# Attention and two dense blocks on one core: scores as three products of rounded parts from the eighth job on

## The chip, the cores and the metric

One core of a Trainium2 chip runs the whole kernel. The metric is the device time of one execution in microseconds (us). The engines are named as the profile names them: PE (TensorE, with its weight loads as PEld), DVE (VectorE), ACT (ScalarE), POOL (GpSimd) and SP (SyncE, which issues most of the transfers). Each engine works through its own instructions in the order in which the program holds them.

## The reference

```python
scores = scale * np.matmul(q, k.transpose(0, 1, 3, 2))        # 4 batches, 8 heads, 576 x 64
thresh = np.max(scores, axis=-1, keepdims=True) - tau
scores = np.where(scores >= thresh, scores, -1000000000.0)
scores = scores - np.max(scores, axis=-1, keepdims=True)
attn = np.exp(scores)
attn = attn / (np.sum(attn, axis=-1, keepdims=True) + 1e-09)
x = np.matmul(attn, v)                                         # then 2304 tokens x 512
h = x @ w_in                                                   # 512 x 2048
g = np.where(h >= 1, h, np.where(h <= -1, 0.0, (h + 1) ** 2 / 4.0))
x = g @ w_out                                                  # 2048 x 512
h = x @ w_in2
out = (h * np.clip(h + 3.0, 0.0, 6.0) / 6.0) @ w_out2
```

All inputs are float32. Which scores pass the threshold depends on small differences between them, so they are computed to nearly full float32 accuracy.

## The kernel before

**Attention.** There are 16 jobs, one for each batch and pair of heads. A job has five blocks of query rows: four of 128 rows, and a last one that holds the 64 remaining rows of both heads. `em_scores` computes a block: for each head and each half of the 576 keys one matmul, whose contraction is the 64 rows of a head, so head 0 uses rows 0 to 63 of the PE array and head 1 rows 64 to 127. These four matmuls (line 328) are plain float32, and the trace records each as two MATMULs. DVE evicts the scores negated, with their maximum (line 341), ACT takes the exponential (line 353), DVE masks and sums (line 362), PE turns the block over by multiplying with the identity (line 277), ACT copies that back (line 390), and PE multiplies with v (line 426).

**q and k.** A matmul wants the 64 head dimensions on the partitions. For the first four jobs (`j < JT`, `JT = 4`) PE turns q and k over, and ACT copies them out of PSUM with the scale (lines 294, 309). From the fifth job on the transfers write strips of 32 elements, so that one DVE transpose of 32 x 32 squares finishes the work (lines 286, 302), and POOL multiplies q by the scale (line 288). `qt` and `kt` have two buffers each, and the scheduler that orders the program places their making a job ahead.

**Dense work.** Matmuls of the dense blocks are three products of rounded parts: an operand is split into `hi` (rounded to the type float32r) and `lo` (the rest, also float32r), and hi·hi, hi·lo and lo·hi are added up in PSUM. Each product is one MATMUL. Weights are loaded as 512 KB tiles (`w_raw`, line 96 and 99) and rounded and split by ACT, DVE and POOL (`split_a`, `split_b`, lines 118 to 141).

**Beside attention.** As soon as the first batch is done, a generator (`part1`) feeds pieces of the first dense block between the pieces of attention: 256 tokens at a time, for the first `NF1 = 10` of 16 inner blocks (lines 666 and 728). Each piece of attention earns `share = 0.57` of credit and a third of a step costs 0.33. The rest of the first block and the whole second block follow after attention, mostly 512 tokens at a time (lines 666 and 708). In attention there are `RAW + MORE = 5` buffers for raw weights.

Of the kernel before, what the change touches and what calls it, by code (L numbers as in the profile page):

```python
# [8 lines left out]
F32 = mybir.dt.float32  # L9
F32R = mybir.dt.float32r  # L10
ACTF = mybir.ActivationFunctionType
ALU = mybir.AluOpType
# [6 lines left out]
def kernel(  # L19
# [13 lines left out]
    V, S, G, T = nc.vector, nc.scalar, nc.gpsimd, nc.tensor  # L33
    NB, NH, SEQ, D = q.shape
# [4 lines left out]
    MAIN = 512  # L39
    TAIL = SEQ - MAIN  # L40
    HS = SEQ // 2
# [3 lines left out]

    WIDE = [MAIN] * NB + [NB * TAIL]
    NW = len(WIDE)
    NF1 = 10
    NAT = 1
    JT = 4  # L50
    MLAG = 2
    RAW = 3
    MORE = 2

    const = ctx.enter_context(tc.tile_pool(name="const", bufs=1))
    wbase = ctx.enter_context(tc.tile_pool(name="wbase", bufs=1))
# [7 lines left out]
    taus = const.tile([128, 4], F32, name="taus")  # L64
# [9 lines left out]
    def f32(ap):  # L74
        return ap.bitcast(F32)
# [26 lines left out]
    def after(ins, prev, sync=False):  # L102
        if prev is not None:
            kind = mybir.DependencyClass.Sync if sync else mybir.DependencyClass.NoSync
            why = mybir.DependencyReason.ANTI if sync else mybir.DependencyReason.DATA
            tc.add_manual_dep(ins.ins, prev.ins.name, mybir.DependencyInfo(kind, why), reason="pace")

    pe_pins = []
    pins = {"S": None, "V": None, "G": None}

    def split_a(kind, m, f):
        t = wraw.pop((kind, m, f))
        pool = wbase if f < NF1 else wpool[f]
        hi = pool.tile([128, 512], F32R, tag=f"w{kind}h{f}", name=f"w{kind}h{f}")
# [91 lines left out]
    ap = att_es.enter_context(tc.tile_pool(name="att", bufs=1))  # L206
    mode = {"mlp": False, "att": True, "step": False, "t": 0, "s": 0, "n": 0}

    qn = ap.tile([128, 5, 128], F32, name="qn")
    kn = ap.tile([128, 5, 128], F32, name="kn")  # L210
    vn = [ap.tile([128, 5, 2, D], F32, name=f"vn{i}") for i in range(2)]
    qt, kt = {}, {}
    rp = ap.tile([128, 32], F32, name="rp")
    rq = ap.tile([128, 32], F32, name="rq")
    G.memset(rp, 0.0)
# [13 lines left out]

    def load_q(j):  # L230
        if j >= NJ:
            return
        E = nc.sync if j else nc.scalar
        b, hp = jobs[j]
        for h in HEADS:
            src = q[b, 2 * hp + h]
            if j >= JT:
                strips(qn, 0, src, h)
                continue
            E.dma_start(out=qn[:, 0:4, h * D:(h + 1) * D], in_=rows(src, b))  # L240
            E.dma_start(out=qn[0:TAIL, 4, h * D:(h + 1) * D], in_=src[MAIN:SEQ, :])

    def load_k(j):
# [23 lines left out]
    readers = {}  # L267
# [5 lines left out]
    def reads(x, ago=0):  # L273
        readers[(mode["s"] - ago) % 2] = x

    def turn(out, in_, pin):
        x = T.transpose(out, in_, ident)  # L277
        if pin:
            pe_pins.append(x)

    def unit_q(j):
        if j >= NJ or j in qt:
            return
        qt[j] = ap.tile([128, SEQ], F32, tag="qt", name="qt", bufs=2)
        if j >= JT:
            V.transpose(out=qt[j], in_=qn.rearrange("p c n -> p (c n)")[:, 0:SEQ])
            load_q(j + 1)
            G.tensor_scalar(out=qt[j], in0=qt[j], scalar1=taus[:, 1:2], scalar2=None, op0=ALU.mult)
            return
        tm = unit_bank().rearrange("p e n -> p (e n)")  # L290
        for c in range(5):
            turn(tm[:, c * 128:(c + 1) * 128], qn[:, c, :], c == 0)
        load_q(j + 1)
        reads(S.activation(out=qt[j], in_=tm[:, 0:SEQ], func=ACTF.Copy, scale=taus[:, 1:2]))

    def unit_k(j):

        if j >= NJ or j in kt:
            return
        kt[j] = ap.tile([128, SEQ + TAIL], F32, tag="kt", name="kt", bufs=2)  # L300
        if j >= JT:
            V.transpose(out=kt[j], in_=kn.rearrange("p c n -> p (c n)"))
            load_k(j + 1)
            return
        tm = unit_bank().rearrange("p e n -> p (e n)")
        for i, c in enumerate((4, 0, 1, 2, 3, 4)):
            turn(tm[:, i * 128:(i + 1) * 128], kn[:, c, :], i == 0)
        load_k(j + 1)
        reads(S.activation(out=kt[j], in_=tm[:, 128 - TAIL:128 + MAIN + TAIL], func=ACTF.Copy))
# [4 lines left out]
    def em_scores(j, i):  # L314

        last = i == NBLK - 1

        if not last:
            mode["s"] += 1
        ss = [unit_bank() for _ in range(1 if last else 2)]  # L320
        prev = None
        c = slice(i * 128, i * 128 + (TAIL if last else 128))
        for x, (h, e) in enumerate(((0, 0), (1, 1), (0, 1), (1, 0)) if last else ((0, 0), (1, 0), (0, 1), (1, 1))):
            r = slice(h * D, (h + 1) * D)
            k0 = e * HS + (TAIL if last or h == 0 else 0)
            o = ss[0][h * TAIL:(h + 1) * TAIL, e, 0:HS] if last else ss[h][:, e, 0:HS]
            with tc.high_priority(offset=900 if x else 0):
                mm = T.matmul(o, qt[j][r, c], kt[j][r, k0:k0 + HS], start=True, stop=True, skip_group_check=True)  # L328
            after(mm, prev)
            prev = mm  # L330
            if x == 0:
                pe_pins.append(mm)
                for y in range(1 if last else 2):
                    after(mm, readers.get((mode["s"] - y) % 2), True)
        nm = ap.tile([128, 2], F32, tag="nm", name="nm", bufs=3)
        th = ap.tile([128, 2], F32, tag="th", name="th", bufs=3)
        p = ap.tile([128, 2, 2, HS], F32, tag="p", name="p", bufs=3)
        if i == 0:
            zt[j] = ap.tile([128, 9], F32, tag="z", name="z", bufs=2)
        for x, s in enumerate(ss):  # L340
            reads(V.tensor_scalar(out=p[:, x], in0=s[:, :, 0:HS], scalar1=-1.0, scalar2=3e38,  # L341
                                           op0=ALU.mult, op1=ALU.min, accum_out=nm[:, x:x + 1]), len(ss) - 1 - x)
        blk[j, i] = (p, nm, th, [])

# [416 lines left out]
    def fin_out(g, a, i):  # L761
# [7 lines left out]
        if c < nmain:  # L769
            b, r = divmod(c, MAIN // 128)  # L770
            if b >= NAT or JT < HP:
                dst = out[b * SEQ + r * 128:b * SEQ + r * 128 + 128, :]
# [5 lines left out]
                b = (c - nmain) * 2 + e  # L778
                nc.sync.dma_start(out=out[b * SEQ + MAIN:(b + 1) * SEQ, :], in_=ob[64 * e:64 * e + 64, :])

    HALF = NF1 // 2
    ROUNDS = [(g, list(range(f, f + HALF))) for f in (0, HALF) for g in range(2)]
    ROUNDS += [(g, list(range(NF1))) for g in range(2, NG)]
    before = {}
    hs = [(r, f) for r, (g, fs) in enumerate(ROUNDS) for f in fs]
    n_h = len(hs)
    outs = [(r, half, f) for r, (g, fs) in enumerate(ROUNDS) for half in range(2) for f in fs]
    OFF = NF1 + 2 * MLAG - 3
    steps, o = [], 0
    while o < len(outs):  # L790
        n = len(steps)
# [94 lines left out]
    V.tensor_scalar(out=taus[:, 3:4], in0=taus[:, 2:3], scalar1=0.0, scalar2=3e38, op0=ALU.is_lt, op1=ALU.mult)  # L886
    V.tensor_scalar(out=taus[:, 1:2], in0=taus[:, 2:3], scalar1=0.0, scalar2=0.125, op0=ALU.is_ge, op1=ALU.mult)
    V.tensor_tensor(out=taus[:, 0:1], in0=taus[:, 2:3], in1=taus[:, 3:4], op=ALU.max)
    warm = [None]

    def warm_up(n):
# [13 lines left out]

    fs1 = list(range(NF1))
    fs2 = list(range(NF1, KF))
    first_use = {("i", f): f for f in fs1}
# [15 lines left out]
            weights.half()  # L924

    part1 = dense1(ready, ahead1)
    share = 0.57
    FIRST, RATE = 5, 0.85
    credit = 0.0
    for _ in attention():  # L930
        if not mode["mlp"]:
            if mode["t"] == 3:
                weights.prefetch()
            if mode["t"] >= 5 and mode["step"]:
                mode["step"] = False
                if weights.done < FIRST and mode["t"] % 5 in (0, 4):
                    weights.half()
            if not ready(0):
                continue
            mode["mlp"] = True  # L940
        credit = min(credit + share, 3.0)
        while credit > 0:
            c = next(part1)
            if c is None:
                break
            credit -= c
# [95 lines left out]
```

## Time and profile before

| | |
|---|---|
| median of 3 runs | 1124.33 us (1123.8 to 1125.87) |
| profiled execution | 1126.53 us, of which the span from the first to the last instruction is 1124.7 us |
| granted TensorE clock, mean | 0.994 of full speed |
| first scores of job 6, 7 and 8 (counted from 0) | about 138, 180 and 218 us |
| first dense matmul beside attention | about 112 us |
| last score matmul, last work of attention | about 457 us, about 477 us |

The span has four parts: attention alone (to 110 us), attention with dense work beside it (to 477 us), the rest of the first dense block (to about 800 us) and the second one. A busy time is the union of an engine's instructions. MATMULs overlap each other, so the time that one takes from the stream is the distance from its start to the next start, and not its own length.

### The profile page before, as it was taken

To read this page: it belongs to the slowest core of one execution; us is meant where nothing else is said; L and a number is where in the kernel's file an instruction comes from. 1 tells how busy PE (TensorE), PEld (TensorE's weight loads), DVE (VectorE), ACT (ScalarE), POOL (GpSimd) and SP (SyncE) were. 2 spreads that over 40 slices of the span, in tenths; PEclk is the share of its full clock that TensorE was granted. 3 is DMA by queue.
4 is the path that set the end of the run, shared out by engine and by line. 5 is a ranking of instruction groups with operands and counts; after the bars stand their busy time and mean duration, and the time that the engine had idled before them with its cause. 6 is when DMAs were issued, how large, how long until landed. Compare 5 with 4: busy or idle time off the path is not lost.

```text
span 1124.7 us, 17618 instructions
## 1 busy us (share of the span) xinstructions
PE 1086.1 (97%) x6478; PEld 881.8 (78%) x6478; DVE 586.9 (52%) x1204; ACT 614.3 (55%) x1215; POOL 435.5 (39%) x382
## 2 busy tenths in 40 slices
PE   7988779999999999999999999999999999999998
PEld 5555557778887778888889888888888888898886
DVE  5788979876666666256535855657410211211111
ACT  5677777776666666565657766645422322333222
POOL 1133667632212221246636666568622222222221
PEclk9999999999999999999999999999999999999999
DMA  6353535433222210015322444543110110010001
GB/s 166 95 117 79 135 102 157 121 73 87 63 59 64 55 39 24 12 49 169 94 85 85 132 147 153 153 128 102 35 38 1 34 38 1 10 38 6 14 1 38
DMA packets 140422, 84.26 MB, mean 75 GB/s; under 512 B 99632, under 2 KB 123440, under 8 KB 140336
## 3 DMA queue, kind: packets, MB, share of 16 engines
q1 hardware_dynamic: 138976, 82.84, 26.8%
q8 instruction: 51, 0.84, 0.3%
q10 hardware_dynamic: 1360, 0.30, 0.1%
q14 instruction: 35, 0.29, 0.1%
HBM read 65.73 MB, written 17.37 MB: 74 GB/s over the span
## 4 chain that ended last, share of the span: by engine, by line
PE 86%; DVE 6%; ACT 3%; DMA 2%; issue 1%; POOL 1%; SPq 1%; ACTq 0%; DVEq 0%; POOLq 0%
PE Q L666 35%; PE P L708 28%; PE Q L728 7%; PE P L328 6%; PE Q L426 5%; PE Q L277 5%; DVE p L341 2%; DVE p L362 2%; ACT e L353 1%; DMA qn<-in_q_dram 1%; DMA w_raw<-in_moe_w_in_dram 0%; DMA rb<-rd 0%; DVE w_c L135 0%; ACT Gf L390 0%; SPq L227 0%
## 5 line engine op out<-in xcount | busy, mean ns | idle before, releaser
L684 POOL TENSOR_TENSOR gl<-r,gh 128x512 fp32r<-128x512 f32 (+1 forms) x190 | 202.4, 1065 | 508.3 <-ACT gh L683 506.4
L666 PE MATMUL Q<-xh,wih 128*128 128x512 f32 (+1 forms) x760 | 262.7, 346 | 6.9 <-DVE r L677 6.0
L666 PE MATMUL Q<-xh,wil 128*128 128x512 f32 (+1 forms) x760 | 257.6, 339 | 0.0
L666 PE MATMUL Q<-xl,wih 128*128 128x512 f32 (+1 forms) x760 | 257.5, 339 | 0.0
L680 DVE SCALAR_TENSOR_TENSOR r<-r,Q 128x512 f32<-128x512 f32 (+1 forms) x80 | 50.7, 634 | 249.3 <-ACT r L679 249.2
L683 ACT ACTIVATE gh<-r 128x512 fp32r<-128x512 f32 (+1 forms) x190 | 99.9, 526 | 128.5 <-PE P L708 52.3
L666 PEld LDWEIGHTS Q<-xh,wih 128*128 128x128 f32 x760 | 144.6, 190 | 31.4 <-DVE r L677 8.2
L666 PEld LDWEIGHTS Q<-xl,wih 128*128 128x128 f32 x760 | 144.6, 190 | 15.8
L666 PEld LDWEIGHTS Q<-xh,wil 128*128 128x128 f32 x760 | 144.5, 190 | 15.3
L341 DVE TENSOR_SCALAR_CACHE_REDUCE p<-P 128x576 f32<-128x576 f32 x144 | 103.9, 751 | 54.4 <-PE Q L277 39.1
L362 DVE SCALAR_TENSOR_TENSOR p<-p,th,e 128x576 f32<-128x576 f32 x144 | 123.6, 879 | 15.4 <-ACT e L353 9.6
L679 ACT ACTIVATE r<-Q,three 128x512 f32<-128x512 f32 (+1 forms) x80 | 51.5, 643 | 143.7 <-PE Q L666 140.5
L353 ACT ACTIVATE e<-p,nm 128x576 f32<-128x576 f32 x144 | 108.5, 774 | 29.2 <-DVE p L341 28.3
L677 DVE SCALAR_TENSOR_TENSOR r<-r,Q 128x256 f32<-128x256 f32 (+1 forms) x110 | 54.9, 499 | 120.2 <-ACT r L676 117.0
L277 PE MATMUL Q<-ident,p 128*128 128x128 f32 x656 | 108.5, 284 | 7.8 <-ACT Gf L390 4.3
L328 PE MATMUL P<-kt,qt 64*128 64x288 f32 (+1 forms) x640 | 99.4, 429 | 14.7 <-DVE p L341 13.8
L708 PE MATMUL P<-woh,gh 128*128 128x512 f32 x288 | 111.9, 390 | 0.6 <-DVE ob L766 0.6
L708 PE MATMUL P<-wol,gh 128*128 128x512 f32 x288 | 112.2, 390 | 0.0
L708 PE MATMUL P<-woh,gl 128*128 128x512 f32 x288 | 111.0, 390 | 0.0
L277 PEld LDWEIGHTS Q<-ident,p 128*128 128x128 f32 x656 | 74.5, 142 | 44.2 <-issue 11.8
L137 POOL TENSOR_TENSOR w_c<-w_c,w_raw 128x512 int32<-128x512 int32 x64 | 88.7, 1387 | 41.7 <-DVE w_c L135 21.8
L390 ACT ACTIVATE Gf<-Q 128x512 f32<-128x512 f32 x128 | 74.2, 595 | 34.4 <-PE Q L277 33.6
(91 smaller groups left out, 1834.3 us busy)
## 6 DMA issues: line engine op xcount, KB each, us to landing
w_raw<-in_moe_w_in_dram SPq DMA_DIRECT2D x32, 512.0 KB
w_raw<-in_moe_w_out_dram SPq DMA_DIRECT2D x32, 512.0 KB
vn<-in_v_dram SPq DMA_DIRECT2D x32, 128.0 KB
x2p<-ob SPq DMA_DIRECT2D x16, 256.0 KB
x2d<-ob SPq DMA_DIRECT2D x16, 256.0 KB
xst<-x2d SPq DMA_DIRECT2D x16, 256.0 KB
out_dram<-ob SPq DMA_DIRECT2D x16, 256.0 KB
xst<-xd SPq DMA_DIRECT2D x15, 256.0 KB
```

The lines of the kernel that those rows point to most:

```text
L137: x = G.tensor_tensor(out=c.bitcast(I32), in0=c.bitcast(I32), in1=r, op=ALU.add)
L277: x = T.transpose(out, in_, ident)
L328: mm = T.matmul(o, qt[j][r, c], kt[j][r, k0:k0 + HS], start=True, stop=True, skip_group_check=True)
L341: reads(V.tensor_scalar(out=p[:, x], in0=s[:, :, 0:HS], scalar1=-1.0, scalar2=3e38, op0=ALU.mult, op1=ALU.min, accum_out=nm[:, x:x + 1]), ...
L353: pins["S"] = S.activation(out=e, in_=p[:, x], func=ACTF.Exp, bias=nm[:, x:x + 1], scale=-1.0)
L362: V.scalar_tensor_tensor(out=p[:, x], in0=p[:, x], scalar=th[:, x:x + 1], in1=e, op0=ALU.is_le, op1=ALU.mult, accum_out=zt[j][:, z:z + 1])
L390: S.activation(out=f[:, h, :, d0:d0 + 128], in_=tm.rearrange("p (c n) -> p c n", c=4), func=ACTF.Copy)
L666: mm = T.matmul(h, l[:, kk * 128:(kk + 1) * 128], r, start=(x == 0), stop=(x == 3 * KD - 1))
L683: x = S.activation(out=gh, in_=r, func=ACTF.Copy)
L684: y = G.tensor_tensor(out=gl, in0=r, in1=f32(gh), op=ALU.subtract)
L708: T.matmul(a, l, r, start=(first and x == 0), stop=(last and x == 2))
L728: mm = T.matmul(o, l, r, start=(f == fs[0] and x == 0 and i == 0), stop=(f == fs[-1] and x == 2 and i == 1), skip_group_check=True)
```

## The change

From the eighth job on (`JT = 7`) the scores are three products too. `split_t` lets DVE transpose the strips into `raw` (one buffer), ACT copy that into the rounded part (`qt`, `kt`, now float32r), and POOL subtract to get `ql` and `kl`. A block then is 12 MATMULs instead of 4 float32 matmuls. The last block of such a job is done for both heads at once: the 64 rows of head 0 and of head 1 stand in q on the diagonal of a 128 x 128 square whose other half is zero, so six MATMULs with all 128 rows do it. The scale moves into the eviction (`scalar1 = taus[:, 3:4]`), and POOL's multiplication falls away. Jobs 4 to 6 (counted from 0) now take the way over PE that jobs 0 to 3 took. Nine inner blocks instead of ten run beside attention, in rounds of 4 and 5, with a share of 0.52, and there is one buffer less for raw weights.

```diff
-    NF1 = 10
+    NF1 = 9
-    JT = 4
+    JT = 7
-    MORE = 2
+    MORE = 1
...
             if j >= JT:
-                strips(qn, 0, src, h)
+                strips(qn, 0, src[0:MAIN, :], h)
+                strips(qn, 16 + 2 * h, src[MAIN:SEQ, :], h)
                 continue
...
+    def split_t(nat, hi, name):
+        raw = ap.tile([128, SEQ + TAIL], F32, tag="raw", name="raw")
+        lo = ap.tile([128, SEQ + TAIL], F32R, tag=name, name=name, bufs=2)
+        V.transpose(out=raw, in_=nat.rearrange("p c n -> p (c n)"))
+        S.activation(out=hi, in_=raw, func=ACTF.Copy)
+        G.tensor_tensor(out=lo, in0=raw, in1=f32(hi), op=ALU.subtract)
+        return lo
...
         if j >= JT:
-            V.transpose(out=qt[j], in_=qn.rearrange("p c n -> p (c n)")[:, 0:SEQ])
+            ql[j] = split_t(qn, qt[j], "ql")
             load_q(j + 1)
-            G.tensor_scalar(out=qt[j], in0=qt[j], scalar1=taus[:, 1:2], scalar2=None, op0=ALU.mult)
             return
...
         if j >= JT:
-            V.transpose(out=kt[j], in_=kn.rearrange("p c n -> p (c n)"))
+            kl[j] = split_t(kn, kt[j], "kl")
...
+        terms = ((qt, kt), (qt, kl), (ql, kt)) if thirds else ((qt, kt),)
+        for pair in (((0, 0),), ((0, 1),)) if whole else (es[0:2], es[2:4]):
+            for n, (a, w) in enumerate(terms):
+                for h, e in pair:
+                    r = slice(0, 128) if whole else slice(h * D, (h + 1) * D)
...
-            reads(V.tensor_scalar(out=p[:, x], in0=s[:, :, 0:HS], scalar1=-1.0, scalar2=3e38,
+            reads(V.tensor_scalar(out=p[:, x], in0=s[:, :, 0:HS],
+                                           scalar1=taus[:, 3:4] if j >= JT else -1.0, scalar2=3e38,
...
-    HALF = NF1 // 2
-    ROUNDS = [(g, list(range(f, f + HALF))) for f in (0, HALF) for g in range(2)]
+    HALF = 4
+    ROUNDS = [(g, list(range(a, z))) for a, z in ((0, HALF), (HALF, NF1)) for g in range(2)]
...
-    share = 0.57
+    share = 0.52
```

**Order on PE.** First block of the eighth job; P are the score banks of the two heads. Before:

```order
L328 MATMUL P_2359<-kt,qt 128x288
L328 MATMUL P_2360<-kt,qt 128x288
L328 MATMUL P_2359<-kt,qt 128x288
L328 MATMUL P_2360<-kt,qt 128x288
L666 MATMUL Q_2073<-xh,wih_1311 128x256
```

Now:

```order
L349 MATMUL P_2357<-kt,qt 128x288
L349 MATMUL P_2358<-kt,qt 128x288
L349 MATMUL P_2357<-kl,qt 128x288
L349 MATMUL P_2358<-kl,qt 128x288
L349 MATMUL P_2357<-kt,ql 128x288
L349 MATMUL P_2358<-kt,ql 128x288
L349 MATMUL P_2357<-kt,qt 128x288
L349 MATMUL P_2358<-kt,qt 128x288
L349 MATMUL P_2357<-kl,qt 128x288
L349 MATMUL P_2358<-kl,qt 128x288
L349 MATMUL P_2357<-kt,ql 128x288
L349 MATMUL P_2358<-kt,ql 128x288
```

The two heads still alternate, and a bank gets its three products one pair after the other.

**Order on DVE.** Around the last block of the eighth job, where q and k of a later job are made (L341 and L364 are evictions, L362 and L386 masks). Before:

```order
L677 SCALAR_TENSOR_TENSOR r<-r,Q_2424 128x256
L356 TENSOR_SCALAR th<-nm,taus 128x2
L362 SCALAR_TENSOR_TENSOR p,z<-p,th,e 128x576 x2
L286 STREAM_TRANSPOSE qt<-qn 128x576
L302 STREAM_TRANSPOSE kt<-kn 128x640
L341 TENSOR_SCALAR p,nm<-P_2709 128x576
```

Now:

```order
L364 TENSOR_SCALAR p,nm<-P_2749,taus 128x576
L701 SCALAR_TENSOR_TENSOR r<-r,Q_2333 128x256
L380 TENSOR_SCALAR th<-nm,taus 128x1
L285 STREAM_TRANSPOSE raw<-kn 128x640
L386 SCALAR_TENSOR_TENSOR p,z<-p,th,e 128x576
```

The transpose of k no longer follows that of q at once: the transpose of q stands before this piece, and the one of k behind the eviction, with the mask behind it.

**Order on POOL.** At that place, for q and k of the same job. Before:

```order
L141 TENSOR_TENSOR wol_2592<-w_c,woh_2591 128x512
L122 TENSOR_SCALAR w_c<-w_c 128x512
L288 TENSOR_SCALAR qt<-qt,taus 128x576
L684 TENSOR_TENSOR gl<-r,gh 128x256
L137 TENSOR_TENSOR w_c<-w_c,w_raw 128x512
```

Now:

```order
L287 TENSOR_TENSOR ql<-raw,qt 128x640
L122 TENSOR_SCALAR w_c<-w_c 128x512
L141 TENSOR_TENSOR wol_2586<-w_c,woh_2585 128x512
L708 TENSOR_TENSOR gl<-r,gh 128x256
L287 TENSOR_TENSOR kl<-raw,kt 128x640
```

Where one multiplication by the scale stood (L288), two subtractions stand, with weight work between them.

## Rows read from the trace of the kernel before

**Rows 1.** The page: busy us (share) of each engine, and the chain's shares by engine.

```profile
PE 1086.1 (97%) x6478; PEld 881.8 (78%) x6478; DVE 586.9 (52%) x1204; ACT 614.3 (55%) x1215; POOL 435.5 (39%) x382
...
PE 86%; DVE 6%; ACT 3%; DMA 2%; issue 1%; POOL 1%; SPq 1%; ACTq 0%; DVEq 0%; POOLq 0%
```

**Rows 2.** Stretches in us: length, busy time (instructions) of PE, PEld, DVE, ACT, POOL; clock, DMA.

```profile
0.00:110.00 110.00, 94.17 (x641) 59.36 (x642) 84.69 (x230) 75.63 (x152) 26.26 (x34) 0.97 0.50 116
110.00:230.00 120.00, 101.96 (x747) 79.57 (x745) 106.33 (x228) 92.42 (x203) 80.40 (x70) 0.97 0.48 124
230.00:430.00 200.00, 199.66 (x1555) 159.37 (x1555) 129.91 (x352) 130.96 (x292) 44.89 (x45) 1.00 0.26 61
```

**Rows 3.** PE in order of time, two blocks of scores: start us, us, what.

```profile
304.66 0.28 PE L728 MATMUL Q<-gh,wol 128*128 128x256 f32 x1
304.87 1.19 PE L328 MATMUL P<-kt,qt 64*64 64x288 f32 x8
305.99 0.66 PE L277 MATMUL Q<-ident,p 128*128 128x128 f32 x4
...
310.43 1.24 PE L328 MATMUL P<-kt,qt 64*128 64x288 f32 x8
...
310.78 0.41 PE L328 MATMUL P<-kt,qt 64*128 64x288 f32 x2
...
311.26 0.41 PE L328 MATMUL P<-kt,qt 64*128 64x288 f32 x2
...
311.60 0.66 PE L277 MATMUL Q<-ident,p 128*128 128x128 f32 x4
```

**Rows 4.** PE in order of time: dense matmuls of 256 and of 512 columns.

```profile
312.22 0.28 PE L666 MATMUL Q<-xl,wih 128*128 128x256 f32 x1
312.34 0.29 PE L666 MATMUL Q<-xh,wil 128*128 128x256 f32 x1
...
900.67 0.39 PE L666 MATMUL Q<-xh,wih 128*128 128x512 f32 x1
...
901.58 0.39 PE L666 MATMUL Q<-xl,wih 128*128 128x512 f32 x1
```

**Rows 5.** PE in order of time: q and k of the fourth job turned over.

```profile
65.58 0.71 PE L277 MATMUL P<-ident,qn 128*128 128x128 f32 x5
66.22 0.66 PE L277 MATMUL Q<-ident,p 128*128 128x128 f32 x4
66.71 0.84 PE L277 MATMUL P<-ident,kn 128*128 128x128 f32 x6
67.39 0.71 PE L277 MATMUL Q<-ident,p 128*128 128x128 f32 x5
```

**Rows 6.** Groups by line and form, whole span: count, busy us, mean ns, idle before.

```profile
L684 POOL TENSOR_TENSOR gl<-r,gh 128x512 fp32r<-128x512 f32 x98 | 131.0, 1338 | 267.9 <-ACT gh L683 267.7
...
L288 POOL TENSOR_SCALAR qt<-qt,taus 128x576 f32<-128x576 f32 x12 | 21.2, 1763 | 9.8 <-DVE qt L286 8.6 <-PE Q L277 1.1
...
L302 DVE STREAM_TRANSPOSE kt<-kn 128x640 f32<-128x640 f32 x12 | 9.7, 808 | 0.0
...
L309 ACT ACTIVATE kt<-P 128x640 f32<-128x640 f32 x4 | 2.9, 714 | 0.0
```

**Rows 7.** One stretch as in rows 2, PE and PEld of line 666 alone, then of line 728.

```profile
110.00:230.00 120.00, 30.81 (x204) 27.40 (x204) 0.97 0.48 124
...
110.00:230.00 120.00, 23.80 (x147) 19.73 (x147) 0.97 0.48 124
```

**Rows 8.** In order of time: ACT, and the chain that ended last, around 146 us.

```profile
146.66 0.67 ACT L118 ACTIVATE w_raw<-w_raw 128x512 int32<-128x512 uint32 x1 [1.25 <-DMA w_raw<-in_moe_w_out_dram]
...
145.08 5.12 DMA w_raw<-in_moe_w_in_dram
```

**Rows 9.** DVE in order of time: two masks of the same size.

```profile
133.48 1.77 DVE L362 SCALAR_TENSOR_TENSOR p<-p,th,e 128x576 f32<-128x576 f32 x1 [0.74 <-ACT e L353]
...
310.13 0.82 DVE L362 SCALAR_TENSOR_TENSOR p<-p,th,e 128x576 f32<-128x576 f32 x1
```

More of the change, by code (lines that the diff above doesn't have):

```diff
@@ L211 @@
     vn = [ap.tile([128, 5, 2, D], F32, name=f"vn{i}") for i in range(2)]
-    qt, kt = {}, {}
+    qt, kt, ql, kl = {}, {}, {}, {}
     rp = ap.tile([128, 32], F32, name="rp")
@@ L283, in unit_q @@
             return
-        qt[j] = ap.tile([128, SEQ], F32, tag="qt", name="qt", bufs=2)
+        qt[j] = ap.tile([128, SEQ + TAIL], F32R if j >= JT else F32, tag="qt", name="qt", bufs=2)
         if j >= JT:
-            V.transpose(out=qt[j], in_=qn.rearrange("p c n -> p (c n)")[:, 0:SEQ])
+            ql[j] = split_t(qn, qt[j], "ql")
             load_q(j + 1)
-            G.tensor_scalar(out=qt[j], in0=qt[j], scalar1=taus[:, 1:2], scalar2=None, op0=ALU.mult)
             return
@@ L293, in unit_q @@
         load_q(j + 1)
-        reads(S.activation(out=qt[j], in_=tm[:, 0:SEQ], func=ACTF.Copy, scale=taus[:, 1:2]))
+        if j == JT - 1:
+            G.memset(qn[0:64, 4, 64:128], 0.0)
+            G.memset(qn[64:128, 4, 0:64], 0.0)
+        reads(S.activation(out=qt[j][:, 0:SEQ], in_=tm[:, 0:SEQ], func=ACTF.Copy, scale=taus[:, 1:2]))
     def unit_k(j):
@@ L299, in unit_k @@
             return
-        kt[j] = ap.tile([128, SEQ + TAIL], F32, tag="kt", name="kt", bufs=2)
+        kt[j] = ap.tile([128, SEQ + TAIL], F32R if j >= JT else F32, tag="kt", name="kt", bufs=2)
         if j >= JT:
-            V.transpose(out=kt[j], in_=kn.rearrange("p c n -> p (c n)"))
+            kl[j] = split_t(kn, kt[j], "kl")
             load_k(j + 1)
@@ L322, in em_scores @@
         c = slice(i * 128, i * 128 + (TAIL if last else 128))
[L323 to L334, printed above, removed]
+        thirds = j >= JT
+        whole = thirds and last
+        es = ((0, 0), (1, 1), (0, 1), (1, 0)) if last else ((0, 0), (1, 0), (0, 1), (1, 1))
+        terms = ((qt, kt), (qt, kl), (ql, kt)) if thirds else ((qt, kt),)
+        x = 0
+        for pair in (((0, 0),), ((0, 1),)) if whole else (es[0:2], es[2:4]):
+            for n, (a, w) in enumerate(terms):
+                for h, e in pair:
+                    r = slice(0, 128) if whole else slice(h * D, (h + 1) * D)
+                    k0 = e * HS + (TAIL if last or h == 0 else 0)
+                    if whole:
+                        o, cs = ss[0][:, e, 0:HS], slice(MAIN, MAIN + 128)
+                    else:
+                        o, cs = ss[0][h * TAIL:(h + 1) * TAIL, e, 0:HS] if last else ss[h][:, e, 0:HS], c
+                    with tc.high_priority(offset=900 if x else 0):
+                        mm = T.matmul(o, a[j][r, cs], w[j][r, k0:k0 + HS], start=(n == 0), stop=(n == len(terms) - 1),
+                                      skip_group_check=True)
+                    after(mm, prev)
+                    prev = mm
+                    if x == 0:
+                        pe_pins.append(mm)
+                        for y in range(1 if last else 2):
+                            after(mm, readers.get((mode["s"] - y) % 2), True)
+                    x += 1
         nm = ap.tile([128, 2], F32, tag="nm", name="nm", bufs=3)
@@ L888 @@
     V.tensor_tensor(out=taus[:, 0:1], in0=taus[:, 2:3], in1=taus[:, 3:4], op=ALU.max)
+    V.tensor_scalar(out=taus[:, 3:4], in0=taus[:, 1:2], scalar1=-1.0, scalar2=None, op0=ALU.mult)
     warm = [None]
@@ L942 @@
         while credit > 0:
-            c = next(part1)
+            c = next(part1, None)
             if c is None:
```

## The prediction

> **What bounds the kernel now.** I read the page first. TensorE (PE) is busy for 97% of the span and has 86% of the chain that ended last, so time is saved where PE gets less to do, but only where PE sets the pace [rows 1]. The view by stretches says where that is. From 230 to 430 us PE is busy for 199.66 of 200 us, and DVE and ACT for 130 and 131: there a microsecond less of PE is a microsecond less of time. From 110 to 230 us, where attention first has dense work beside it, PE stands idle for 18.0 of 120 us, while DVE is busy for 106.3. Before 110 us PE is idle for 15.8 [rows 2]. In those two stretches less PE work is worth little, and more DVE work costs.
>
> The change touches the last 9 of 16 jobs, and the second of them starts at about 218 us, so nearly all of its score blocks lie where PE sets the pace.
>
> **What a block of scores costs now.** In order of time, a block of 128 rows starts at 310.43 us, and the next work starts at 311.60, so the block takes 1.17 us of PE [rows 3]. Inside stand four pairs of MATMULs, at 310.43, 310.78, (311.02) and 311.26: the two records of a pair are the two heads, which run side by side, each on half of the array's rows. The step between even pairs is 0.24 us, half of the 0.48 from 310.78 to 311.26. Four such steps are 0.97 us; the other 0.20 us lie at the edges, where the array goes from 128 rows to two halves and back [rows 3]. The last block takes 1.12 us (304.87 to 305.99), and the dense MATMUL ahead of it has a step of 0.21 us, where 0.12 is usual [rows 3, 4].
>
> **What it will cost.** Now each pair is one pass of rounded parts. The trace has no such pass on 64 rows, but it has them on 128: 0.12 us for 256 columns, and 0.2275 for 512 (900.67 to 901.58 holds four) [rows 4]. The difference is 0.1075 us for 256 columns, so 288 columns take 0.12 + 0.0134 = 0.133 us. My choice is that the halves still run side by side, as the float32 pairs do, so a pair takes 0.133. The bounds are 0.121 (half of a float32 step, which has two passes) and 0.267 (one after the other).
>
> The edges are told by a rule too. The Trainium skill, page "TensorEngine Tiling (Array Packing)", section Tiling Modes, says that a change of the tiling mode drains the engine; the 0.20 us at the edges agree. By it the edges stay for blocks on halves and vanish for a block with all 128 rows, which is what I take from the rows as well.
>
> - **Blocks of 128 rows, 36 of them:** 6 x 0.133 + 0.20 = 1.00 us instead of 1.17, so -0.17 each, **-6.2 us**. (With 0.121: 0.93, -8.8.)
> - **Last blocks, 9 of them:** six MATMULs with all 128 rows, without a change of mode: 0.80 us instead of 1.12 + 0.09. -0.41 each, **-3.7 us**.
> - **One inner block less beside attention:** the order holds 144 MATMULs of 256 columns less and 72 of 512 columns more. 144 x 0.12 = 17.3 us against 72 x 0.2275 = 16.4 [rows 4]: **-0.9 us**.
> - **q and k of jobs 4 to 6 over PE:** five and six transposes take 0.64 us (65.58 to 66.22) and 0.68 us (66.71 to 67.39), 1.32 for a job, 4.0 for three [rows 5]. They fall ahead of the third of these jobs, which starts at about 138 us, and there PE is idle for part of the time [rows 2], so part of it costs nothing: I take a third, **+1.3 us** (0 to 4.0). In return DVE loses six transposes of 0.8 us and POOL three multiplications of 1.76, and ACT gets two copies of about 0.71 for each job [rows 6].
> - **A smaller share:** 0.52 instead of 0.57 takes 8.8% of the dense work out of each piece of attention. Between 110 and 230 us that work is 30.8 + 23.8 = 54.6 us of PE [rows 7], so 4.8 us move behind 230 us. If PE set the pace there, the stretch would shrink by as much. But DVE does, and it loses little: the raw weights are split at the same blocks of attention as before. I take **+3.0 us** (0 to 4.8).
>
> **What is hidden.** The parts of q and k now need a DVE transpose (0.81), an ACT copy (0.71) and a POOL subtraction (1.34 for 512 columns, so about 1.67 for 640) [rows 6]: 3.2 us in a row, each twice for a job. In the order they stand a whole job ahead of the scores that read them, and a job is five blocks of some 5.6 us (304.87 to 310.43) [rows 3], so PE doesn't wait for them. The order shows what does wait. There is one `raw`, so DVE's transpose of k waits until POOL has subtracted q's part, and the mask stands behind it. After 230 us DVE is idle for 70 of 200 us [rows 2], which covers some 2.4 us for each job; without that cover it would be 9 x 2.4 = 21.6 us. ACT's 18 copies (12.8 us) are covered by its 69 us of idle time in the same stretch. SP issues four more small transfers of q for a job, a job ahead as well. The scale in the eviction changes a constant into a column, at the same length. One raw buffer less for weights I cost at nothing, since only the time from 110 to 230 us could show it (a rival, below).
>
> **The sum.** -6.2 - 3.7 - 0.9 + 1.3 + 3.0 = -6.5 us. The profiled execution took 1126.53 us (a span of 1124.7 and 1.8 around it), so it would take 1120.0. It lies 2.2 us above the median of the runs, 1124.33. So I expect 1117.8, **1118 us**. With the good ends of all terms (pairs at 0.121, which make the last blocks 0.73 us and -4.4, and nothing lost) it is -14.1 us, about 1110; with the bad ends short of the halves running in turn (+4.0 and +4.8) -2.0 us, about 1122.
>
> **Rivals.**
>
> 1. *The halves don't run side by side with rounded parts.* Then 12 passes of 0.133 follow each other: 1.60 + 0.20 = 1.80 us a block, +0.63 instead of -0.17 for 36 blocks, 28.8 us more: **1147 us**, slower. It decides from a step of 0.163 us for a pair on: there 6 x 0.163 + 0.20 eats up the whole gain. For it speaks only that the trace has no rounded pass on 64 rows; against it, that float32 pairs run side by side in every block [rows 3]. Chance 0.12.
> 2. *Raw weights come late.* With five buffers ACT already waits 1.25 us for a tile at 146.66, and the tile after it, issued at 145.08, takes 5.12 us to land and is on the chain; ACT's queue, with the exponentials, stands behind such a wait [rows 8]. With four buffers a load is issued one tile later. If two more loads are on the chain with 4 us each, it is +7 to +8: **1125 us**, no change. Against it: a smaller share also asks for weights more slowly. Chance 0.17.
> 3. *DVE pays, from 110 to 230 us.* The same wait of DVE for POOL (0.71 + 1.67 = 2.4 us) falls there about five times, for parts of jobs 7 to 9, and there DVE has 13.7 us of idle time in 120 [rows 2, 6]. Beside that, a mask took 1.77 us while POOL worked, and 0.82 elsewhere [rows 9], and POOL gets 30 us of subtractions for its 21.2 us of multiplications [rows 6]. Five waits that no idle time covers are +12: **1130 us**, slower; it decides where more than 6 us stay uncovered. Chance 0.10. The Trainium skill, page "SBUF — State Buffer", section on the two sides of SBUF, says why a mask is longer then: DVE instructions with two SBUF inputs and GpSimd share a port that one of them holds for a whole instruction. By that rule 18 subtractions could hold up DVE for at most 30 us, of which the multiplications that go would have held 21; the mask of 1.77 us agrees with it.
>
> **How the numbers follow.** My forecast, 1110 to 1122, has 0.58. Rival 2 has 0.17, rival 3 0.10, rival 1 0.12, and 0.03 is left for a larger gain, if the stretch up to 230 us gets shorter too. A measurement of this kernel can tell about 0.2% (2.2 us) from no change: below 1122.1 is faster, above 1126.6 slower. Faster gets 0.58, the 0.03, and 0.04 of rival 2: 0.65. The same gets 0.10 of rival 2 and 0.02 of the edge of the third: 0.12. Slower gets the rest, 0.23. The range must leave out no more than 0.2: 1109 to 1131 holds the forecast, rival 2 and most of rival 3, and leaves out rival 1.
>
> **What would show it.** In the profile of the changed kernel, after about 230 us: a block of scores of 12 MATMULs takes 1.0 us from its first start to the next work, its records in pairs with a step of 0.13; the last block takes 0.8 us, and the MATMUL ahead of it has a step of 0.12. PE stays busy in that stretch, and the stretch from the first dense matmul to the end of attention, 365 us long now, is some 25 us shorter, of which 17 us come back after attention. Idle time of PE between 110 and 230 us stays near 18 us, and ACT waits for `w_raw` no longer than before. I am wrong if the records of a block start one by one (rival 1), if ACT's waits for weights grow (rival 2), or if DVE is idle ahead of its transposes for POOL and PE ahead of its scores for DVE (rival 3).

## The result, and the profile after

The changed kernel takes 1130.64 us (median of six runs, 1127.21 to 1133.64), and the kernel before 1125.1 in the same series: a ratio of 1.0053 (95% interval 1.0038 to 1.0067). It is slower by half a per cent, where 1118 us and faster was forecast. The profiled execution, the second longest of the six, took 1133.11 us, of which 1131.3 are its span.

The page of the changed kernel, as [rows 1]:

```profile
PE 1085.6 (96%) x6565; PEld 894.2 (79%) x6565; DVE 593.8 (52%) x1198; ACT 629.2 (56%) x1230; POOL 443.0 (39%) x385
...
PE 76%; DVE 8%; ACT 5%; POOL 4%; DMA 3%; issue 3%; SPq 1%; ACTq 0%; DVEq 0%; POOLq 0%
```

PE is busy as long as before, but its share of the chain that ended last fell from 86% to 76%. More often now it is another engine that the end waits for. The stretches, as [rows 2], say where (length, busy time of PE, PEld, DVE, ACT and POOL, granted clock, DMA):

```profile
0.00:110.00 110.00, 95.31 (x657) 61.17 (x658) 81.92 (x227) 77.30 (x154) 22.54 (x32) 0.97 0.43 107
110.00:230.00 120.00, 100.76 (x727) 78.69 (x726) 102.33 (x214) 91.43 (x196) 74.39 (x65) 0.91 0.48 119
230.00:430.00 200.00, 196.51 (x1678) 168.52 (x1678) 143.42 (x374) 143.82 (x315) 54.46 (x51) 0.99 0.27 64
...
480.00:600.00 120.00, 115.80 (x637) 99.49 (x636) 64.80 (x85) 73.42 (x136) 73.38 (x60) 1.00 0.36 112
```

Three things differ from before. From 110 to 230 us PE is idle for about as long (19.2 us, 18.0 before), but the granted clock is 0.91 and was 0.97, some 7 us of this stretch. From 230 to 430 us, where PE had hardly stopped, it is now idle for 3.5 us. And behind attention, from 480 to 600 us, it is idle for 4.2 us; the same stretch of the kernel before reads

```profile
480.00:600.00 120.00, 119.98 (x655) 104.18 (x654) 61.14 (x84) 69.95 (x133) 63.29 (x52) 1.00 0.31 96
```

with POOL busy for 63 us, and 73 now.

The blocks of scores themselves came out as forecast. PE in order of time in the changed kernel, a last block and a block of 128 rows, as [rows 3]:

```profile
303.72 0.28 PE L752 MATMUL Q<-gh,wol 128*128 128x256 f32 x1
303.84 0.30 PE L349 MATMUL P<-kt,qt 128*128 128x288 f32 x1
303.97 0.30 PE L349 MATMUL P<-kl,qt 128*128 128x288 f32 x1
...
304.65 0.27 PE L278 MATMUL Q<-ident,p 128*128 128x128 f32 x1
...
307.42 0.40 PE L349 MATMUL P<-kt,qt 64*128 64x288 f32 x2
307.66 0.30 PE L349 MATMUL P<-kl,qt 64*128 64x288 f32 x2
307.80 0.30 PE L349 MATMUL P<-kt,ql 64*128 64x288 f32 x2
...
308.20 0.29 PE L349 MATMUL P<-kt,ql 64*128 64x288 f32 x2
308.42 0.39 PE L690 MATMUL Q<-xh,wih 128*128 128x256 f32 x1
```

The block of 128 rows takes 308.42 - 307.42 = 1.00 us; its records come in pairs (x2) with a step of 0.13 to 0.14, and 0.24 and 0.22 at the edges. The last block takes 0.81 us, and the step ahead of it is 0.12. So the work that PE had to lose it lost, and the question is what gave it back.

One place behind 230 us shows how. The changed kernel, all engines in order of time (PEld and some rows left out; in brackets the idle time before, and what ended it):

```profile
360.86 1.57 POOL L287 TENSOR_TENSOR ql<-raw,qt 128x640 fp32r<-128x640 f32 x1 [5.26 <-PE Q L690]
...
363.51 0.83 DVE L285 STREAM_TRANSPOSE raw<-kn 128x640 f32<-128x640 f32 x1
...
364.27 0.38 DVE L674 TENSOR_TENSOR xl<-xu,xh 128x256 fp32r<-128x256 f32 x1
...
365.19 1.58 POOL L287 TENSOR_TENSOR kl<-raw,kt 128x640 fp32r<-128x640 f32 x1 [1.89 <-ACT kt L286]
...
365.31 1.75 DVE L674 TENSOR_TENSOR xl<-xu,xh 128x256 fp32r<-128x256 f32 x1
...
367.05 0.41 DVE L701 SCALAR_TENSOR_TENSOR r<-r,Q 128x256 f32<-128x256 f32 x1
...
367.49 0.42 ACT L707 ACTIVATE gh<-r 128x256 fp32r<-128x256 f32 x1 [2.07 <-DVE r L701]
...
367.81 0.37 ACT L456 ACTIVATE xu<-Q 128x256 f32<-128x256 f32 x1
...
368.23 1.11 PE L278 MATMUL Q<-ident,p 128*128 128x128 f32 x4 [2.40 <-ACT xu L456]
...
369.36 0.41 PE L690 MATMUL Q<-xl,wih 128*128 128x256 f32 x1
369.57 0.41 PE L690 MATMUL Q<-xh,wil 128*128 128x256 f32 x1
...
371.44 0.29 PE L690 MATMUL Q<-xh,wil 128*128 128x256 f32 x1
371.56 0.28 PE L752 MATMUL Q<-gh,woh 128*128 128x256 f32 x1
```

Read it backwards from PE's stop of 2.40 us. PE waits for a PSUM bank that ACT frees with `xu`; on ACT `xu` stands in order behind `gh`, which waits 2.07 us for DVE's `r`; DVE is late because an `xl` beside POOL's `kl` took 1.75 us, where the same form took 0.38 us a moment earlier. And the stop has a second price: when PE goes on, its dense steps are 0.21 us until about 371.4, and 0.12 after that. The stretches around it show the granted clock (behind the busy times of the five engines):

```profile
355.00:367.00 12.00, 10.84 (x97) 9.02 (x96) 9.79 (x21) 8.13 (x19) 4.62 (x4) 1.00 0.22 51
367.00:371.00 4.00, 2.77 (x13) 2.77 (x14) 3.22 (x11) 2.53 (x5) 0.73 (x1) 0.62 0.14 22
371.00:379.00 8.00, 8.00 (x71) 7.70 (x70) 6.15 (x16) 5.31 (x13) 0.75 (x1) 0.98 0.28 82
```

0.62 over 4 us is three quarters of the time at the lower level, 1.2 GHz.

### The profile page after: what moved, and what is told of

The parts are those of the page before. It is cut to its first block, busy times and chain, and to the rows that moved or that the text cites. A ratio compares the mean times of both kernels' runs of the same rounds, so it can differ in the third digit from the quotient of the medians.

```text
span 1131.3 us, 17848 instructions
## 1 busy us (share of the span) xinstructions
PE 1085.6 (96%) x6565; PEld 894.2 (79%) x6565; DVE 593.8 (52%) x1198; ACT 629.2 (56%) x1230; POOL 443.0 (39%) x385
## 4 chain that ended last, share of the span: by engine, by line
PE 76%; DVE 8%; ACT 5%; POOL 4%; DMA 3%; issue 3%; SPq 1%; ACTq 0%; DVEq 0%; POOLq 0%
PE Q L690 30%; PE P L732 25%; PE Q L450 6%; PE Q L752 5%; PE P L349 5%; PE Q L278 5%; DVE p L386 2%; DVE p L364 2%; POOL w_c L137 2%; ACT e L377 1%; DVE w_c L135 1%; DMA xst<-xd 1%; DVE w_c L129 1%; ACT Gf L414 1%; DVE xl L674 1%
## 5 line engine op out<-in xcount | busy, mean ns | idle before, releaser
L386 DVE SCALAR_TENSOR_TENSOR p<-p,th,e 128x576 f32<-128x576 f32 x144 | 127.1, 904 | 16.2 <-ACT e L377 10.1
L349 PE MATMUL P<-kt,qt 64*128 64x288 f32 (+2 forms) x442 | 76.8, 410 | 6.6 <-DVE p L364 5.8
L364 DVE TENSOR_SCALAR_CACHE_REDUCE p<-P,taus 128x576 f32<-128x576 f32 x81 | 63.3, 813 | 30.1 <-PE Q L278 26.0
```

The costliest lines, as they stand in the source:

```text
L349: mm = T.matmul(o, a[j][r, cs], w[j][r, k0:k0 + HS], start=(n == 0), stop=(n == len(terms) - 1), skip_group_check=True)
L386: V.scalar_tensor_tensor(out=p[:, x], in0=p[:, x], scalar=th[:, x:x + 1], in1=e, op0=ALU.is_le, op1=ALU.mult, accum_out=zt[j][:, z:z + 1])
```

## The experiments

**Theory A:** the shorter score blocks bring their 10 us, and three other things take them and 5 more: the tenth block's weights, split behind attention now; the making of the parts (DVE's wait for POOL, and the column in the eviction); and the lower clock behind the stops. **Theory B:** nine blocks, PE's q and k and four buffers carry the whole loss, and the split is free. Ratios are to the kernel before in the same series; its median was 1125.1 beside the changed kernel and 1124.66 to 1124.89 in the three series of the experiments. By the intervals, the difference of two rows is known to about 2 us. In `no_subtract` and `const_nosub` the rounded part stands in for the remainder, and in `pool_other` the remainder is zero: these three leave a part of the result out and tell only of time.

| kernel | us | ratio, 95% interval |
|---|---|---|
| changed kernel | 1130.64 | 1.0053 (1.0038 to 1.0067) |
| `nine_only` | 1128.06 | 1.0030 (1.0020 to 1.0040) |
| `pe7_only` | 1128.34 | 1.0028 (1.0016 to 1.0040) |
| `nine_pe7_raw4` | 1129.54 | 1.0038 (1.0024 to 1.0052) |
| `share57` | 1130.68 | 1.0051 (1.0037 to 1.0066) |
| `no_subtract` | 1123.32 | 0.9988 (0.9975 to 1.0000) |
| `pool_other` | 1126.50 | 1.0012 (1.0002 to 1.0022) |
| `minus_dve` | 1125.86 | 1.0005 (0.9993 to 1.0016) |
| `constant` | 1126.93 | 1.0014 (1.0005 to 1.0024) |
| `late_const` | 1126.93 | 1.0012 (1.0001 to 1.0023) |
| `const_nosub` | 1118.58 | 0.9944 (0.9922 to 0.9966) |
| `const_dve` | 1121.12 | 0.9968 (0.9958 to 0.9977) |
| `const_dve_gl` | 1116.59 | 0.9924 (0.9911 to 0.9937) |

**The parts around the three products.** `nine_only` is the kernel before with nine blocks and the share of 0.52:

```diff
-    NF1 = 10
+    NF1 = 9
...
-    share = 0.57
+    share = 0.52
...
```

> The kernel before with nine inner blocks beside attention (rounds of four and five) and the share of 0.52, and nothing else of the change: float32 scores, over PE for jobs 0 to 3, five raw buffers. Theory A (three causes share the loss: nine blocks, the waits of the split, the clock): the weights of the tenth block are now split after attention, and PE waits there for POOL some 5 us more; with the moved work (-0.9 and +3.0 of the prediction) 1125 + 2.1 + 5.6 = about 1132. Theory B (nine blocks with PE's q and k and four buffers carry the whole loss, and the split is free): 1133 to 1137. The terms of the prediction alone: 1127.

It measured 3.4 us more than before: less than the 7 to 8 of theory A, more than the 2.1 of the prediction. Its stretch behind attention shows PE idle for 3.6 us and POOL busy for 73; between 470 and 610 us PE waits 2.1 us for POOL's `gl` and once 1.3 us for DVE's `r`:

```profile
480.00:600.00 120.00, 116.40 (x657) 100.91 (x656) 64.64 (x85) 75.09 (x140) 73.37 (x60) 1.00 0.36 115
```

`pe7_only` is the kernel before with `JT = 7` alone, and `nine_pe7_raw4` is `nine_only` with both of these lines, and float32 scores throughout:

```diff
-    JT = 4
+    JT = 7
-    MORE = 2
+    MORE = 1
```

> The kernel before with q and k over PE up to job 6 instead of job 3, and nothing else of the change. The prediction took +1.3 us (0 to 4.0); with four raw buffers in addition it was 1.5 us. By the prediction's term: 1126. If the four buffers were what cost the 1.5: 1125, as before.

> All of the change but the three products: nine blocks, share 0.52, q and k over PE up to job 6, four raw buffers; scores stay float32 from the first job to the last, with no split. Against it the changed kernel shows what the three products and their split bring by themselves. Theory A: they bring less than the 10 us that the score blocks got shorter by, about 3 us, since waits and a lower clock take the rest: 1131 + 3 = 1134. Theory B: they bring the whole 10 us, and this kernel takes about 1141. Rival C (the split costs more than it saves): below 1131.

PE's q and k by themselves cost 3.4 us, more than either expectation (1126 or 1125); together with four buffers, on top of nine blocks, they cost 1.5 more (1129.54 against 1128.06), which the intervals don't tell from nothing. All parts around the three products cost 4.9 us. Theory B falls: it wanted 1141. Theory A's 1134 is missed too: 1129.54 lies below 1131, where rival C put it. So the three products, whose blocks got 10 us shorter, brought nothing in the changed kernel: 1130.64 against 1129.54, with intervals that overlap.

`share57` is the changed kernel with one line put back:

```diff
-    share = 0.52
+    share = 0.57
```

> The changed kernel with the share of 0.57 as before. The prediction took +3.0 us (0 to 4.8) for the smaller share: by that term this is about 1128. If DVE, ACT and POOL bound the stretch from 110 to 230 us entirely, more dense work there only lets PE wait, and it stays at 1130 to 1131. Theory A says between: 1129.

It takes the same time as the changed kernel, which the expectation gave for the case that DVE, ACT and POOL bound the stretch up to 230 us; theory A's 1129 is missed. In the changed kernel the share costs nothing. On the kernel before it wasn't tried by itself, so `nine_only` holds it together with the nine blocks.

**What takes the gain.** `no_subtract` is the changed kernel without the subtraction on POOL, and `pool_other` has it, but reading no `raw`:

```diff
-        lo = ap.tile([128, SEQ + TAIL], F32R, tag=name, name=name, bufs=2)
...
-        G.tensor_tensor(out=lo, in0=raw, in1=f32(hi), op=ALU.subtract)
-        return lo
+        return hi
```

```diff
-        G.tensor_tensor(out=lo, in0=raw, in1=f32(hi), op=ALU.subtract)
+        G.tensor_tensor(out=lo, in0=f32(hi), in1=f32(hi), op=ALU.subtract)
```

> The changed kernel without the subtraction on POOL: the rounded part stands in for the remainder in the second and third product, so all MATMULs are issued, DVE still transposes and ACT still copies, but nothing waits for POOL and POOL has 18 subtractions less. Theory A (waits for POOL, and its contention with DVE, cost 5 to 8 us): about 1124 to 1126. Theory B (the split is free): 1130 to 1131, as the changed kernel.

> The changed kernel with POOL's subtraction of the same size, but reading the rounded part twice instead of raw, so the remainder is left out (it is zero): POOL works as long as before and DVE's next transpose doesn't wait for it any more. Without the subtraction it was 1123. Theory W (the 7 us come from DVE's wait for the one raw buffer): 1123 to 1125. Theory P (they come from POOL's time itself, its queue and the slower DVE instructions beside it): 1129 to 1131.

The subtraction is worth 7.3 us, below what theory A had. In `pool_other` 4.1 of them are gone, with DVE's wait for `raw`; the other 3.2 need POOL at work. So it is neither theory W nor P alone. The two aren't cleanly parted, though: the expectation took POOL to work as long as before, but reading one tile twice its subtraction takes 1.25 us in the median, and 1.57 in the changed kernel, so the 4.1 us hold that shorter work too. The wait as it stands in the changed kernel, DVE in order of time:

```profile
215.09 0.20 DVE L380 TENSOR_SCALAR th<-nm,taus 128x1 f32<-128x1 f32 x1
217.07 0.85 DVE L285 STREAM_TRANSPOSE raw<-kn 128x640 f32<-128x640 f32 x1 [1.77 <-POOL ql L287]
217.84 1.64 DVE L386 SCALAR_TENSOR_TENSOR p<-p,th,e 128x576 f32<-128x576 f32 x1
```

DVE stands for 1.77 us until POOL has done q's part, and the mask behind it takes 1.64 us, beside POOL again. From 217.07 on DVE has no pause, and the delay reaches PE (some rows left out):

```profile
220.03 1.72 POOL L287 TENSOR_TENSOR kl<-raw,kt 128x640 fp32r<-128x640 f32 x1
220.27 1.51 DVE L469 TENSOR_SCALAR z<-z 128x9 f32<-128x9 f32 x1
...
222.15 0.36 DVE L674 TENSOR_TENSOR xl<-xu,xh 128x256 fp32r<-128x256 f32 x1
...
222.60 0.39 ACT L456 ACTIVATE xu<-Q 128x256 f32<-128x256 f32 x1 [1.76 <-DVE xl L674]
...
223.04 0.66 PE L278 MATMUL Q<-ident,p 128*128 128x128 f32 x4 [2.22 <-ACT xu L456]
...
223.65 0.28 PE L752 MATMUL Q<-gl,woh 128*128 128x256 f32 x1
223.77 0.28 PE L752 MATMUL Q<-gh,wol 128*128 128x256 f32 x1
```

An operation on nine columns takes 1.51 us beside POOL's `kl` (at 366.98 it took 0.16), DVE's `xl` comes late, ACT's `xu` waits for it, and PE stops for 2.22 us. What POOL's work does to DVE is in the mean of `xl` from 230 to 460 us (fifteen of one form in each), in the changed kernel and in `minus_dve`, where POOL doesn't subtract:

```profile
L674 DVE TENSOR_TENSOR xl<-xu,xh 128x256 fp32r<-128x256 f32 x15 | 8.7, 596 | 0.8 <-ACT xh L673 0.8
```

```profile
L674 DVE TENSOR_TENSOR xl<-xu,xh 128x256 fp32r<-128x256 f32 x15 | 5.8, 409 | 0.0
```

`minus_dve` subtracts on DVE:

```diff
-        G.tensor_tensor(out=lo, in0=raw, in1=f32(hi), op=ALU.subtract)
+        V.tensor_tensor(out=lo, in0=raw, in1=f32(hi), op=ALU.subtract)
```

> The changed kernel with the 18 subtractions on DVE, behind its transpose on the same engine, instead of on POOL. DVE gets some 0.9 us for each, 16 us in all, POOL loses 28. Theory P or W (POOL's part, its wait or its contention, is what costs): 1124 to 1127. Rival D (DVE's own load is what counts, most of all up to 230 us): 1131 or more.

It takes 4.8 us less than the changed kernel, in the range of theories P and W, though DVE has eighteen instructions more, of 0.82 us in the median and at most 1.91. So rival D is out, and POOL's part costs more than the same work on DVE; against no subtraction at all (1123.32) the work on DVE costs 2.5 us. The Trainium skill, page "SBUF — State Buffer", section on the two sides of SBUF, says that DVE instructions with two SBUF inputs and GpSimd share a port that one of them holds for its whole instruction. The trace of the changed kernel agrees: POOL's `kl` ends at 365.19 + 1.58 = 366.77 us, and the `xl` that started 0.12 us after it at 365.31 + 1.75 = 367.06, so it got its 0.3 us when POOL was done.

`constant` gives the eviction a constant and lets ACT's copies carry the test of tau (as a factor of 1 or 0):

```diff
-        S.activation(out=hi, in_=raw, func=ACTF.Copy)
+        S.activation(out=hi, in_=raw, func=ACTF.Copy, scale=taus[:, 3:4])
...
-                                           scalar1=taus[:, 3:4] if j >= JT else -1.0, scalar2=3e38,
+                                           scalar1=-0.125 if j >= JT else -1.0, scalar2=3e38,
...
-    V.tensor_scalar(out=taus[:, 3:4], in0=taus[:, 1:2], scalar1=-1.0, scalar2=None, op0=ALU.mult)
+    V.tensor_scalar(out=taus[:, 3:4], in0=taus[:, 1:2], scalar1=8.0, scalar2=None, op0=ALU.mult)
```

> The changed kernel with a constant in the eviction again: ACT's copies of q and k multiply by 1 (or by 0 for a negative tau), and DVE evicts with -0.125 instead of a column. 81 evictions took 0.813 us with the column and 0.750 with the constant, so DVE loses 5.1 us of work. Theory A (DVE stands on the path where dense work first lies beside attention, and PE waits for each eviction there): 2 to 5 us less than the changed kernel, 1126 to 1128.5. Rival (PE sets the pace, the eviction is hidden): 1130 to 1131.

It takes 3.7 us less, as theory A had it. The groups of the eviction from 230 to 460 us, with the column (changed kernel) and with the constant:

```profile
L364 DVE TENSOR_SCALAR_CACHE_REDUCE p<-P,taus 128x576 f32<-128x576 f32 x70 | 54.7, 814 | 29.2 <-PE Q L278 25.1 <-PE P L349 3.6
```

```profile
L364 DVE TENSOR_SCALAR_CACHE_REDUCE p<-P 128x576 f32<-128x576 f32 x68 | 49.1, 753 | 34.1 <-PE Q L278 29.5 <-PE P L349 4.5
```

One thing the runs don't hold still: the scheduler gives each version its own order. At the place of the stop at 368 us, `constant` reads

```profile
361.48 1.79 DVE L674 TENSOR_TENSOR xl<-xu,xh 128x256 fp32r<-128x256 f32 x1
361.58 0.36 ACT L456 ACTIVATE xu<-Q 128x256 f32<-128x256 f32 x1
...
363.91 0.42 ACT L707 ACTIVATE gh<-r 128x256 fp32r<-128x256 f32 x1 [1.96 <-DVE r L701]
363.93 0.38 PE L690 MATMUL Q<-xh,wih 128*128 128x256 f32 x1 [1.27 <-DVE r L701]
```

The `xl` beside POOL is as long as before, but ACT's `xu` stands ahead of `gh`, and PE stops for 1.27 us instead of 2.40. So the 3.7 us are what the edit brought together with its order. What the length of the eviction alone would bring isn't shown, and the same holds for the other runs.

`late_const` is `constant` with DVE's transposes from job 4 as before, and the three products only from job 9 (cut to its core):

```diff
-    JT = 7
+    JT = 4
+    TH = 9
...
-        thirds = j >= JT
+        thirds = j >= TH
```

> Nine blocks, the share of 0.52 and four raw buffers as in the changed kernel, DVE's transposes from job 4 as before, the three products only from job 9, with the constant in the eviction. Seven of nine jobs keep the gain, 7 x 1.1 = 7.7 us, against 1128 to 1130 for the kernels without it. Theory A (the split costs where DVE is the bound, up to 250 us, and little later): 1121 to 1123. Rival (each split costs the same wherever it lies, some 0.8 us a job): 1126 to 1128.

It takes as long as `constant`, in the range of its rival. Two jobs less have the gain and the split, and q and k of jobs 4 to 6 are off PE again, so the run mixes two changes; but it doesn't bear out theory A's guess that the split is cheap once DVE is no longer the bound. The stop at 368 us lies in that later part too.

`const_nosub` joins the edits of `constant` and `no_subtract`:

> The changed kernel with the constant in the eviction and without POOL's subtraction (the remainder is left out, the rounded part stands in for it). By itself the constant brought 3.7 us and the missing subtraction 7.3. Theory A (the column and the subtraction are separate costs, and with both gone the whole gain of the shorter score blocks, some 10 us against the 1129.5 of the kernel without three products, is there): 1119 to 1120. Rival (both are the same wait of PE, counted twice): 1122 to 1123, as with the subtraction alone gone.

It takes 1118.58 us, 11.0 less than `nine_pe7_raw4`, just below theory A's 1119 to 1120: with the column and the subtraction gone, the whole gain of the score blocks is there, although DVE's transposes and ACT's copies remain. So those were hidden. From the first dense MATMUL to the last one with v, first `nine_pe7_raw4`, then the changed kernel, then `const_nosub` (one profiled execution each):

```profile
111.10:460.10 349.00, 334.80 (x2563) 263.29 (x2561) 246.95 (x622) 242.77 (x535) 121.48 (x114) 0.99 0.31 78
```

```profile
114.30:466.80 352.50, 331.36 (x2688) 276.76 (x2688) 257.41 (x623) 253.81 (x553) 134.66 (x125) 0.97 0.32 77
```

```profile
113.40:452.60 339.20, 323.83 (x2689) 271.32 (x2688) 243.63 (x623) 253.59 (x553) 104.91 (x107) 0.99 0.32 80
```

PE is idle for 14.2, 21.1 and 15.4 us. What the clock took (one minus the clock, times the length) is about 3, 11 and 3 us, each known to about 2, since the clock is printed to 0.01. Without both, the three come to about 331, 321 and 320 us: the three products save 10 or 11 us of PE at full speed in both kernels that have them, and in the changed one stops and the clock take them back.

How much each of them takes isn't to be read from these executions alone. That of `nine_pe7_raw4` is its shortest of seven (1126.61 us, mean clock 0.997), that of the changed kernel the second longest of six (1133.11, 0.986). By the mean clock of every run (one minus the clock, times the span, medians) the clock took 11.9 us in the changed kernel, 9.0 in `nine_pe7_raw4` and 6.2 in `const_nosub`. Without it their medians come to 1118.8, 1120.5 and 1112.4 us. So of the lost gain about 6 us are stops, and about 3 (against `nine_pe7_raw4`) to 6 (against `const_nosub`) are the clock.

**A version that beats both.** `const_dve` joins the edits of `constant` and `minus_dve`; `const_dve_gl` also moves `gl` to DVE behind attention, while weights of the first layer are still split:

```diff
-        y = G.tensor_tensor(out=gl, in0=r, in1=f32(gh), op=ALU.subtract)
+        if not mode["att"] and weights.done < 2 * KF:
+            vlast, y = V.tensor_tensor(out=gl, in0=r, in1=f32(gh), op=ALU.subtract), pins["G"]
+        else:
+            y = G.tensor_tensor(out=gl, in0=r, in1=f32(gh), op=ALU.subtract)
```

> The changed kernel with the constant in the eviction and the 18 subtractions on DVE; the whole result is computed. By themselves the constant brought 3.7 us and the move to DVE 4.8. Theory A (they add up): about 1122. Rival D (DVE becomes the bound with 16 us more, and takes back what the constant gives): 1125 to 1127.

> As the kernel with the constant and the subtractions on DVE, and behind attention gl, as long as weights of the first layer are still split, on DVE instead of POOL. With nine blocks PE stands idle for 3.6 us of the 120 behind attention, most of it ahead of the second product for POOL's gl; with ten it was 0.02. Theory A (POOL, with one more block of weights to split, is late there): 3 us less than without this edit. Rival (DVE, busy for 16 of 20 us at 510 to 530, is late in its place): no less.

The first takes 1121.12 us, so the two add up. The second takes 1116.59, 0.76% less than the kernel before: 4.5 us for `gl`, more than the 3 expected. The kernel before has little to win there: with ten blocks PE is idle for 0.02 us of that stretch. PE's stretch behind attention in the second, where the first has 117.27 us of PE and 73.29 of POOL:

```profile
480.00:600.00 120.00, 119.64 (x709) 106.64 (x708) 72.17 (x106) 79.49 (x151) 60.85 (x52) 1.00 0.36 115
```

## Why the prediction was wrong

The forecast, 1118 us and faster, failed, though 1130.64 us still lies at the upper edge of the range of 1109 to 1131, which held most of rival 3. Two steps failed: the subtraction of the parts counted as hidden, and the column counted at the length of a constant. In a sum they account for the miss: 7.3 + 3.7 us that the prediction put at nothing, 1.3 more for the nine blocks with the smaller share (3.4 instead of 2.1) and 0.2 more for q and k, so -6.5 becomes +6.0; measured are +5.5.

- **Blocks of 128 rows (-6.2) and last blocks (-3.7): right.** 1.00 and 0.81 us for the forecast 1.00 and 0.80. The halves run side by side; rival 1 (1147 us) is out. `const_nosub` has the whole gain in its time (11.0 us for 9.9).
- **"The scale in the eviction changes a constant into a column, at the same length": a step that failed.** The column takes 0.813 us instead of 0.753, 81 times, and putting the constant back brought 3.7 us, with its order. The trace of before had no eviction with a column beside it to read that from, so it should have had bounds, as the other unknown costs had.
- **The split as hidden: the main step that failed.** The prediction let DVE's idle time of 70 us behind 230 us cover its wait for `raw`, and put nothing for DVE instructions that get longer beside POOL. An average of idle time covers nothing for the instruction that is next in order: 2 us on DVE pass through ACT's queue to a PSUM bank of PE, as at 217 and at 365 us. POOL's subtraction cost 7.3 us, up to 4.1 of them by the wait. The transposes and ACT's copies were hidden, as forecast: with them `const_nosub` has the whole gain.
- **Rival 3 (DVE pays, 1130 us, chance 0.10) comes closest.** Its mechanism, the one `raw` buffer and DVE instructions that get longer beside POOL, is borne out by `pool_other` and `minus_dve`. Its place, 110 to 230 us, was too narrow: in the profiled execution that stretch lost 1.2 us more to stops and some 7 to the clock, which the rival didn't name, and the stretch behind it 3.2 us to stops. Its 12 us for the waits were 7.3 for all of the subtraction. That its time came out right is luck: the eviction and the stretch behind attention, which it didn't name either, made up the rest.
- **One inner block less (-0.9): mis-sized.** It counted PE's columns alone. The block's weights moved with it, to where POOL also makes `gl`, and PE waits there: `nine_only` measured +3.4 (with the smaller share), and `gl` on DVE gave 4.5 back.
- **A smaller share (+3.0): zero in the changed kernel.** `share57` takes the same time.
- **q and k over PE (+1.3, 0 to 4.0):** 3.4 alone, and 1.5 on top of nine blocks with the fourth buffer, both inside the bounds.
- **Rival 2 (raw weights late):** four buffers are inside those 1.5 us, so they don't cost the 7 to 8 us that it needs. Up to 480 us ACT waits 2.1 us for `w_raw`, and 1.2 before.
- **The clock was in no term.** At 368 us a stop of PE was paid twice, by itself and by the lower level behind it. Over all runs the clock took some 3 us more than in `nine_pe7_raw4`, about half of what the stops took.
- **A sign that failed:** the stretch from the first dense MATMUL to the end of attention was to be 25 us shorter than 365; in the profiled execution it is 352.5.

What stays open: how the 7.3 us of the subtraction divide into DVE's wait, POOL's queue, longer DVE instructions and the clock, and what share of each difference comes from the order that the scheduler gave the version. And not every stop is followed by the lower level: behind the stop of 2.22 us at 223 us the steps are 0.12, and so they are in `constant` behind its stop of 1.27 us.

## What to carry to other kernels

Before calling work on a side engine hidden, follow one instance to the bottleneck: which instruction stands next in order behind the late one, which buffer it frees, and whether TensorE waits for that. When a block of work is moved past a stage, move everything that makes its operands in the sum too, and look at how busy those engines are where it lands. A single buffer between two engines, and a constant that becomes a column, are costs to bound from both sides and not zeros.

## What the runs showed of the hardware

- A DVE eviction of 128 x 576 from PSUM with a column as its factor took 0.814 us, with a constant 0.753 (means from 230 to 460 us).
- Float32r MATMULs on 64 rows run side by side in pairs, with a step of 0.13 us for 288 columns.
- Behind PE's stop of 2.40 us the granted clock was at the lower level: steps of 0.21 us instead of 0.12 until 371.4. Behind one of 2.22 us in the same execution the steps stayed at 0.12. The time of the six runs of the changed kernel follows their clock: the one with a mean clock of 0.993 took 1127.21 us, those with 0.986 took 1133.11 and 1133.64.
- A DVE subtraction of 128 x 256 that took 0.38 us alone took 1.75 us beside a POOL subtraction of 1.58.
- A POOL subtraction of 128 x 640 took 1.57 us in the median with two different tiles, and 1.25 with the same tile twice.
